# Attention followed by a maxout layer: AV with stationary exponentials, transposes by DMA, six banks for scores, batch 0 in halves

## The chip, the cores and the metric

The kernel runs on one core of one Trainium2 chip. The metric is the time of one execution on the device in microseconds (us). Executions of a kernel are told as the median of the runs. A run more than 1.5% above the fastest of its kernel counts as slow, and comparisons are made between fast runs. Engines: PE is TensorE (matmuls), PEld its weight loads, DVE is VectorE, ACT is ScalarE, POOL is GpSimd, SP is SyncE, which issues DMAs here. "Granted clock" is the share of TensorE's full clock that the throttle let through.

## The reference

```python
# q, k, v: (8, 12, 448, 64) float32
scores = (1 / sqrt(64)) * q @ k^T
m = max(scores);  e = exp(scores - m)
attn = e / (sum(e) + exp(-m) + 1e-9)       # but for the 1e-9: exp(s) / (sum exp(s) + 1)
x = (attn @ v) -> (8*448, 12*64) = (3584, 768)
h = max(x @ w1, x @ w2, x @ w3)            # three 768 x 768 weights
out = h @ w_out                            # (3584, 768) float32
```

## The kernel before

The work is cut into 24 groups of four heads (three groups to a batch). For each group q and k are loaded, transposed on PE, multiplied to scores (keys on partitions, 112 a chunk), and exponentiated on ACT. The exponentials `eT` are the moving operand of AV: four heads sit side by side in 32-column tiles of the PE array. The denominator is a third such product, with ones as weights. Up pieces (a 128x448 tile of `x @ w_i`) and output pieces of the batch before are put between the visits of attention to keep PE busy.

```python
def pair_qk(i):                     # DVE: two heads side by side, for the transposes
    ...
        nc.vector.tensor_copy(out=k16, in_=kf[...]); nc.vector.tensor_copy(out=q16, in_=qf[...])

def transpose_pair(i, pr):          # PE: 8 transposes into a PSUM bank, DVE copies them out
    trT = ps1.tile([128, 2, S], MMDT, tag="bank1", name="trT")
    for n, t16 in enumerate((k16, q16)):
        for c in range(NCH):
            nc.tensor.transpose(out=trT[:, n, ts(c, SC)], in_=t16[:, c, :, :], ...)
    nc.vector.tensor_copy(out=qkT, in_=trT.rearrange("p n s -> p (n s)"))

def av_group(i):
    def col_tiled(weights):         # 16 matmuls, four heads at once in column tiles of 32
        for c in range(NCH):
            for hh in range(GH):
                nc.tensor.matmul(out=bank[32*hh : 32*hh+32, 0:S], lhsT=weights(hh, c),
                                 rhs=eT[:, hh, c, :], start=(c == 0), stop=(c == NCH - 1))
    den = col_tiled(lambda hh, c: ones16[:, :])
    nc.scalar.activation(out=lnd, in_=den[:, 0:S], func=AF.Ln, bias=one_b)
    nc.scalar.activation(out=rb, in_=lnd, func=AF.Exp, bias=ln_lam, scale=-1.0)
    for hf in range(2):
        num = col_tiled(lambda hh, c: v16[:, hh, c, hf::2])
        nc.vector.tensor_tensor(out=xT[b][:, 2*g + hf, :], in0=num[:, 0:S], in1=rb, op=ALU.mult)
...
# PSUM: ps1 = 4 banks (AV, transposes, up, output), ps2 = 2 x 2 banks (scores)
for i in range(NI):                 # 24 groups, four visits each
    ...
    for vi, (pr, cs) in enumerate(visits):
        scores_visit(i, pr, cs)
        # visit 0: up/output pieces, av_group(i - 1), pieces, pair_qk(i + 1)
        # visits 1, 2: pieces, transpose_pair(i + 1, vi - 1), pieces;  visit 3: pieces
```

The softmax here doesn't subtract the row's maximum and nothing guards it: scores larger than these inputs give would overflow.

## Time and profile before

| | before |
|---|---|
| median of the first three runs | 379.88 us |
| PE busy | 358.3 us of a 377.6 us span |
| ACT busy, DVE busy | 194.5 us, 194.7 us |
| time for one group, first AV to first AV, mean of 19 | 14.6 us |

The head of the profile's page of the kernel before: the span, then busy time and share of the span by engine.

```profile
span 377.6 us, 7320 instructions
PE 358.3 (95%) x3120; PEld 172.0 (46%) x3120; DVE 194.7 (52%) x395; ACT 194.5 (52%) x241; POOL 59.4 (16%) x92
```

PE is the bound. The view by windows of the kernel before tells where it is not. The columns are the stretch, then busy time and number of instructions of each engine, the granted clock, the DMA share and GB/s.

```profile
core 0: us, PE busy (x) PEld busy (x) DVE busy (x) ACT busy (x) POOL busy (x), PEclk, DMA share, GB/s
0.00:40.00 40.00, 26.18 (x269) 11.64 (x270) 12.08 (x33) 27.48 (x35) 20.76 (x37) 1.00 1.12 175
...
120.00:160.00 40.00, 40.00 (x364) 18.88 (x360) 22.18 (x46) 22.51 (x29) 6.29 (x9) 1.00 0.49 83
...
350.00:378.00 28.00, 22.91 (x128) 12.18 (x126) 13.16 (x22) 0.00 (x0) 0.00 (x0) 0.98 0.20 57
```

(The DMA share adds up the times of packets and can pass 1.) Outside the first 40 us and the last 28 PE has no idle time to give; only less PE work, or an earlier start, can shorten the kernel. What one group costs on PE is read from the timeline of the kernel before, PE only (start, time until the last of the merged matmuls ends, line, output and inputs, count):

```profile
135.20 1.30 PE L220 MATMUL p_i<-xT,w_124 128*128 128x448 f16 x6
136.34 1.30 PE L220 MATMUL p_i<-xT,w_122 128*128 128x448 f16 x6
137.57 0.55 PE L161 MATMUL stp<-qkT 64*128 64x448 f16 x4
138.05 0.94 PE L190 MATMUL av<-eT,ones_116 112*32 112x448 f16 x16
138.81 1.69 PE L190 MATMUL av<-eT,ld_v 112*32 112x448 f16 x32
140.43 1.31 PE L220 MATMUL p_i<-xT,w_123 128*128 128x448 f16 x6
```

Differences of starts are what counts, as the pipelined ends overlap: six up matmuls take 136.34 - 135.20 = 1.14 us, the AV burst of 48 takes 140.43 - 138.05 = 2.38 us. An up piece that a score visit follows holds PE for 1.23 us (137.57 - 136.34), 0.09 more; there PE changes from the whole array to row tiles.

### The profile page before, as it was taken

The numbers are of one execution on the slowest core, as the hardware profiler recorded it, in microseconds if no ns is written. First come the engines' busy times: TensorE is split into PE (matmuls) and PEld (weight loads), VectorE is DVE, ScalarE is ACT, GpSimd is POOL, SyncE is SP. The second block draws the span as 40 slices with busy tenths as digits, with TensorE's granted clock in tenths as the row PEclk, the third lists the DMA queues.
The fourth block names the chain that finished last, engine by engine and source line by source line (L and its number), as shares of the span: only waits on it lengthen the run. The fifth ranks groups of instructions, "written<-read, shape, count | busy, mean of one in ns | idle before, by whom it ended". The sixth has DMA issues, their size and how long they took to land.

```text
span 377.6 us, 7320 instructions
## 1 busy us (share of the span) xinstructions
PE 358.3 (95%) x3120; PEld 172.0 (46%) x3120; DVE 194.7 (52%) x395; ACT 194.5 (52%) x241; POOL 59.4 (16%) x92
## 2 busy tenths in 40 slices
PE   2777999999999999999999999999999999999995
PEld 1233444544445444454445544454444554445552
DVE  2233545545546546546546555455465465445553
ACT  1879464663655655555555645546555554552000
POOL 8533450220210201202202202202000000000000
PEclk9999999999999999999999999999999999999999
DMA  7999998555508625455236555077010410013005
GB/s 92 185 208 206 204 196 121 73 136 68 73 2 151 111 54 75 60 139 75 32 43 89 126 101 73 6 128 141 2 26 0 128 43 0 2 32 95 2 0 168
DMA packets 40064, 32.71 MB, mean 87 GB/s; under 512 B 2272, under 2 KB 35296, under 8 KB 40032
## 3 DMA queue, kind: packets, MB, share of 16 engines
q0 software_dynamic: 35552, 21.24, 40.8%
q1 hardware_dynamic: 4480, 11.01, 9.8%
q8 instruction: 24, 0.39, 0.5%
q14 instruction: 8, 0.07, 0.0%
HBM read 42.47 MB, written 11.01 MB: 142 GB/s over the span
## 4 chain that ended last, share of the span: by engine, by line
PE 84%; DMA 9%; ACT 2%; POOL 2%; DVE 1%; issue 1%; DVEq 0%; POOLq 0%
PE p_i L220 43%; PE op_ps L241 15%; PE av L190 11%; PE stp L161 10%; PE trT L144 4%; DMA w_123<-in_moe_w_dram 3%; DMA ld_k<-in_k_dram 3%; DMA ld_q<-in_q_dram 2%; DVE xT L206 1%; ACT eT L170 1%; ACT rb L203 1%; ACT lnd L201 1%; POOL ld_q L88 1%; POOL ld_k L88 1%; POOL ld_v L88 0%
## 5 line engine op out<-in xcount | busy, mean ns | idle before, releaser
L170 ACT ACTIVATE eT<-stp 112x896 f16<-112x896 f32 x192 | 164.9, 916 | 145.1 <-PE stp L161 145.1
L230 DVE TENSOR_TENSOR hT<-hT,p_i 128x448 f16<-128x448 f16 x96 | 59.4, 619 | 45.5 <-PE p_i L220 45.1
L206 DVE TENSOR_TENSOR xT<-av,rb 128x448 f16<-128x448 f32 x48 | 27.8, 619 | 70.8 <-ACT rb L203 64.7
L220 PE MATMUL p_i<-xT,w_122 128*128 128x448 f16 x288 | 63.0, 353 | 0.4
L220 PE MATMUL p_i<-xT,w_123 128*128 128x448 f16 x288 | 62.4, 353 | 0.0
L220 PE MATMUL p_i<-xT,w_124 128*128 128x448 f16 x288 | 62.2, 353 | 0.0
L161 PE MATMUL stp<-qkT 64*128 64x448 f16 x384 | 56.3, 364 | 4.9 <-ACT eT L170 4.8
L241 PE MATMUL op_ps<-w_125,hT 128*128 128x384 f16 x336 | 59.5, 326 | 0.0
L88 POOL DMA_DIRECT2D ld_v<-in_v_dram x24 | 16.8, 702 | 192.3 <-PE av L190 126.3
L248 DVE TENSOR_SCALAR o_sb<-op_ps 128x384 f32<-128x384 f32 x56 | 31.2, 557 | 28.5 <-PE op_ps L241 28.4
L241 PEld LDWEIGHTS <-hT 128*128 128x128 f16 x336 | 30.9, 98 | 24.8 <-issue 6.3
L190 PE MATMUL av<-eT,ld_v 112*32 112x448 f16 x768 | 41.8, 361 | 0.0
L228 DVE CAST hT<-p_i 128x448 f16<-128x448 f32 x48 | 29.7, 620 | 19.9 <-PE p_i L220 19.9
L220 PEld LDWEIGHTS <-w_123 128*128 128x128 f16 x288 | 25.9, 98 | 29.6 <-issue 9.2
L220 PEld LDWEIGHTS <-w_124 128*128 128x128 f16 x288 | 26.0, 98 | 28.7 <-issue 7.8
L220 PEld LDWEIGHTS <-w_122 128*128 128x128 f16 x288 | 26.1, 98 | 27.8 <-issue 7.0
L149 DVE COPY qkT<-trT 128x896 f16<-128x896 f16 x48 | 29.5, 615 | 3.1 <-PE trT L144 3.0
L161 PEld LDWEIGHTS <-qkT 64*128 64x128 f16 x384 | 12.0, 94 | 40.9 <-issue 40.3
L190 PEld LDWEIGHTS <-ld_v 112*32 112x32 f16 x768 | 21.0, 99 | 16.8 <-issue 1.7
L190 PE MATMUL av<-eT,ones_116 112*32 112x448 f16 x384 | 23.3, 364 | 0.0
L88 POOL DMA_DIRECT2D ld_q<-in_q_dram x25 | 17.7, 709 | 6.9 <-DMA w_124<-in_moe_w_dram 1.5
L88 POOL DMA_DIRECT2D ld_k<-in_k_dram x25 | 17.6, 703 | 4.4 <-DMA w_123<-in_moe_w_dram 1.1
(305 smaller groups left out, 142.1 us busy)
## 6 DMA issues: line engine op xcount, KB each, us to landing
ld_v<-in_v_dram POOLq DMA_DIRECT2D x24, 224.0 KB, 4.0
ld_q<-in_q_dram POOLq DMA_DIRECT2D x23, 224.0 KB, 4.9
ld_k<-in_k_dram POOLq DMA_DIRECT2D x23, 224.0 KB, 5.9
out_dram<-o_sb SPq DMA_DIRECT2D x8, 336.0 KB, 2.8
out_dram<-o_sb SPq DMA_DIRECT2D x8, 288.0 KB, 2.7
out_dram<-o_sb SPq DMA_DIRECT2D x8, 240.0 KB, 2.8
out_dram<-o_sb SPq DMA_DIRECT2D x8, 192.0 KB, 2.7
w_122<-in_moe_w_dram POOLq DMA_DIRECT2D x3, 384.0 KB, 10.7
```

Source lines behind the costliest of these rows:

```text
L88: nc.gpsimd.dma_start(out=tiles[name][:, h0 : h0 + step].rearrange("p h c d -> p h (c d)"), in_=src[:, h0 : h0 + step],)
L144: nc.tensor.transpose(out=trT[:, n, ts(c, SC)], in_=t16[:, c, :, :], identity=ident16[0:SC, 0:SC],)
L149: nc.vector.tensor_copy(out=qkT, in_=trT.rearrange("p n s -> p (n s)"))
L161: nc.tensor.matmul(out=stp[:, hh, 0:S], lhsT=qkT[hh * D : hh * D + D, c * SC : c * SC + 128], rhs=qkT[hh * D : hh * D + D, S : 2 * S], sta ...
L170: nc.scalar.activation(out=st["eT"][:, 2 * pr : 2 * pr + 2, c, :], in_=stp[0:SC, :, 0:S], func=AF.Exp, scale=scale,)
L190: nc.tensor.matmul(out=bank[32 * hh : 32 * hh + 32, 0:S], lhsT=weights(hh, c), rhs=eT[:, hh, c, :], start=(c == 0), stop=(c == NCH - 1),)
L206: nc.vector.tensor_tensor(out=xT[b][:, 2 * g + hf, :], in0=num[:, 0:S], in1=rb, op=ALU.mult)
L220: nc.tensor.matmul(out=p_i[:, 0:S], lhsT=w_sb[i][:, dc, ts(fc, 128)], rhs=xT[b][:, dc, :], start=(dc == 0), stop=(dc == NDC - 1),)
L228: nc.vector.tensor_copy(out=dst, in_=p_i[:, 0:S])
L230: nc.vector.tensor_tensor(out=dst, in0=dst, in1=p_i[:, 0:S], op=ALU.max)
L241: nc.tensor.matmul(out=op_ps[:, 0:NW], lhsT=hT[bp][:, fc, ts(t, 128)], rhs=wout_sb[:, fc, ts(nh, NW)], start=(fc == 0), stop=(fc == NFC - 1),)
L248: nc.vector.tensor_scalar(out=o_sb[:, ts(nh, NW)], in0=op_ps[:, 0:NW], scalar1=1.0 / LAMBDA, scalar2=None, op0=ALU.mult,)
```

## The change

The intent: take work from PE and shorten the start.

- AV with the exponentials stationary (113 or 112 rows, 128 columns) and v moving, with a 65th value column of constants that gives the denominator, and a 113th row of ones that gives its "+ 1". DVE takes reciprocals and multiplies; ACT loses Ln and Exp.
- AV's result now has queries on partitions, so x must be transposed as well. From group 5 on q and k, and from group 3 on x, are transposed by DMAs issued on SP.
- The pairing copies of q and k go from DVE to POOL, and POOL copies v into the widened buffer.
- PSUM: three score tiles of two banks (AV uses them too), two single banks for all else; three score visits a group for four.
- Batch 0 is done in query halves, so that its up pieces can start earlier.

```diff
-    ps1 = ... bufs=4 ...
-    ps2 = ... bufs=2 ...
+    ps_s = ctx.enter_context(tc.tile_pool(name="ps_s", bufs=3, space=bass.MemoryType.PSUM))
+    ps_b = ctx.enter_context(tc.tile_pool(name="ps_b", bufs=2, space=bass.MemoryType.PSUM))
 ...
+    def transpose_dma(i):
+        for pr in range(GH // 2):
+            t = att_pool.tile([2 * D, 2 * S], MMDT, tag="qkT", name="qkT")
+            for n in range(2):                       # k, then q
+                nc.sync.dma_start_transpose(
+                    out=t[:, n * S : (n + 1) * S].rearrange("p (c r) -> p c r", c=NCH),
+                    in_=paired[i][pr][n].rearrange("p c h d -> p (c h d)"),
+                )
+    def prep_v(i):
+        nc.gpsimd.tensor_copy(out=v_buf[i % NE][0:SC, :, :, 0:D], in_=raw[i].pop("v"))
 ...
+    def av(i, pr, qcs=(0, 1, 2, 3)):
 ...
+                    nc.tensor.matmul(
+                        out=ps[:, hh, j * (D + 1) : (j + 1) * (D + 1)],
+                        lhsT=eF[0:kk, o : o + 128],
+                        rhs=vx[0:kk, h, c, 0 : D + 1],
+                        start=(c == 0), stop=(c == NCH - 1),
+                    )
+        nc.vector.reciprocal(out=rb[:, :, 0:nq], in_=acc[:, :, :, D])
+        nc.vector.tensor_tensor(out=xn[i][...], in0=acc[:, :, :, 0:D], in1=rb[...], op=ALU.mult)
 ...
+    def x_transpose_dma(i):
+        nc.sync.dma_start_transpose(out=xt_tile(b)[...], in_=xn[i].rearrange("p a j h d -> p (a j h d)"))
 ...
+        for vi, units in enumerate(visits):          # three visits, groups 4 to 23
+            scores(i, units)
 ...
+                fill(per / 6)
+                if vi < 2:
+                    av(i - 1, vi)
+                if vi == 1:
+                    x_transpose_dma(i - 1)
+                    if i + 1 < NI and i + 1 >= PE_QK:
+                        transpose_dma(i + 1)
+                fill(per / 6)
```

The last lines: in each group, SP is given the x transpose of the group whose AV has just been issued, and the four transposes that the next group's scores need.

## The prediction

> **What bounds the kernel now.** TensorE. The page gives PE 95% busy of 377.6 us; the window table shows PE busy for all but 0.2 us of each 40 us between 80 and 320 us, at full granted clock. Only the first 40 us are loose (PE 26.2 us busy, ScalarE 27.5, DMA share above 1). The chain of waits is PE for 84%, DMA 9% (its start).
>
> A group of four heads takes 14.6 us (distance of successive AV bursts in the chain). From start-to-start times in the PE timeline: 36 up matmuls at 0.189 us = 6.8; 14 output matmuls at 0.1625 = 2.3; 8 row-tiled score pairs at 0.189 = 1.5; the AV burst 2.4 (48 column-tiled matmuls, four at once); 16 transposes at 0.049 = 0.8; and about 0.1 us each time PE changes between full array and tiles, near 0.8 a group. 24 groups: about 350 us.
>
> **What changes (estimates from those durations).**
> 1. AV: 48 wide matmuls a group become 64 with 128 stationary columns and 65 moving ones. A weight load with a 112-column transpose matmul takes 48.5 ns in the trace, the load hidden, so a pair costs at most that; streaming alone would be some 29 ns. The Trainium skill ("TensorE: Matmul & The Clock Gate", "Back-to-back issue gap") states a floor near 25 ns, but 81 ns for 128-column pairs; this trace contradicts the second. I take 34 ns: 2.2 us a group for 2.3. AV itself hardly pays.
> 2. DMA transposes for groups 5 to 23 remove 19 x 0.8 = 15 us from PE, the critical engine, and two 0.62 us VectorE copies a group.
> 3. Full-array AV and three score visits for four: 9 mode changes become 6: 6 us.
> 4. ScalarE loses Ln and Exp (31 us), VectorE the pair copies (to GpSimd): off the critical path, slack only.
> 5. Batch 0 in halves: up work starts near 22 to 25 us instead of 39. But DMA moved at most about 2 MB per 9.4 us slice, so the second weight lands near 30 us, the third near 35. I expect 6 to 10 us gained; PE dense from about 35 us.
> 6. The ring for up and output pieces falls from four banks to two; a piece takes 1.14 us, its eviction 0.62 plus about 0.3: just enough. I allow 6 us of stalls.
>
> PE work is then about 331 us, plus some 9 us of idle at the start, 5 at the end, 6 of stalls.
>
> **Predicted: 350 us, 8 in 10 between 334 and 369. Faster by over 2%: 0.89; within 2%: 0.07; slower: 0.04.**
>
> **What would show it.** A group period near 13.4 us (13.1 if AV pairs run at 30 ns, 14.3 at 48). AV burst of 64 near 2.2 us. No PE transposes after about 40 us. ScalarE near 166 us, its waits all for PE. First up matmul at 22 to 26 us, its wait ended by a weight DMA.
>
> **What would make it wrong.**
> - AV pairs slower than 45 ns: 15 to 25 us lost.
> - DMA transposes: some 0.69 MB a group in 256-byte rows. At the 261 GB/s of the skill's "DMA: Bandwidth & Descriptors" ("Latency and other measured facts") that is 2.6 us, hidden; no trace shows it yet. Before's packets of about 600 bytes took about 69 ns; if each row cost that, transposes and loads would fill the 16 engines for over a group's period, PE would wait on the transposed q, k or x, and the time would be 370 or more.
> - GpSimd copies late, delaying the transposes.
> - Two banks too few: PE waits for VectorE at every piece.
> - Batch 0 waiting longer for weights.

## The result

| | before | after |
|---|---|---|
| median of 6 runs | 379.76 us | 423.12 us |
| median of the 4 fast runs of after | | 420.90 us |
| span of the profiled run | 377.6 us | 421.8 us |
| PE busy | 358.3 us | 355.0 us |
| PE not busy | 19.3 us | 66.8 us |
| mean granted clock | 0.999 | 0.949 |
| time for one group | 14.6 us | 15.8 us (first scores to first scores, mean of 14) |

The ratio is 1.108 (95% interval 1.102 to 1.114). Ratios here are the mean time of one kernel's fast runs over that of the other's of the same rounds, so not quite the ratio of the medians quoted. Two of the six runs of after counted as slow by their time (424.36 and 427.52 us); the profiled one is fast. Differences to after are taken from 420.90 below; the expectations took 423.

The record of the clock begins at 21.9 us in before and at 24.2 us in after, and the mean counts the time ahead of it as full speed. In after it was not: eight score matmuls of 224 columns take 0.93 us at 20.9 us and 0.56 at 26.1. So clocks are compared from 80 us on.

The page of the kernel after: span and busy times, then its chain of waits by engine.

```profile
span 421.8 us, 8277 instructions
PE 355.0 (84%) x3438; PEld 203.7 (48%) x3438; DVE 181.5 (43%) x343; ACT 165.0 (39%) x193; POOL 133.4 (32%) x200
...
PE 64%; DMA 21%; SPq 7%; DVE 3%; issue 2%; POOL 1%; ACT 1%; ACTq 0%; POOLq 0%
```

PE is busy for almost as long as before, though it was given less work. The windows of the kernel after:

```profile
0.00:40.00 40.00, 21.47 (x265) 12.76 (x266) 14.80 (x37) 13.30 (x15) 26.46 (x43) 0.89 1.15 172
80.00:120.00 40.00, 29.61 (x295) 18.11 (x296) 11.57 (x22) 16.46 (x20) 16.29 (x24) 0.83 0.66 109
120.00:160.00 40.00, 36.90 (x346) 20.18 (x345) 18.29 (x33) 18.81 (x23) 12.76 (x19) 1.00 0.70 114
...
280.00:320.00 40.00, 31.85 (x278) 16.48 (x277) 15.03 (x27) 15.50 (x19) 13.07 (x20) 0.93 0.75 114
```

There is idle time in every stretch, and in some the clock is down. The list of waits of the kernel after (engine and what waited, on what, us in all, times, longest) says for what:

```profile
PE stp L207 <- DMA qkT<-q: 38.8, 19, 5.3
...
PE avp L237 <- POOL vx L194: 11.9, 2, 8.7
```

Score matmuls of all 19 groups that use DMA transposes wait for a transposed q: 38.8 us. The first AV matmuls of batch 0 wait 11.9 us for POOL's copies of v. The timeline of the kernel after over one change of group shows how the first comes about:

```profile
136.42 1.21 PE L237 MATMUL avp<-vx,e 113*128 113x65 f16 x32
...
137.91 0.69 DVE L249 TENSOR_TENSOR xn<-avp,rb 112x512 f16<-112x512 f32 x1
138.63 1.22 SPq L277 DMA_TRANSPOSE xT<-xn  x1
...
139.96 1.20 SPq L186 DMA_TRANSPOSE qkT<-k  x1
141.25 1.21 SPq L186 DMA_TRANSPOSE qkT<-q  x1
142.57 1.20 SPq L186 DMA_TRANSPOSE qkT<-k  x1
143.67 0.74 PE L207 MATMUL stp<-qkT 64*128 64x448 f16 x6 [0.91 <-DMA qkT<-q]
```

The x transpose starts 0.03 us after DVE has made its input. Behind it each issue holds SP for 1.2 us, and the q that the next scores need lands 2.4 us after its issue. From the end of AV's matmuls (136.42 + 1.21) to the scores 6.0 us pass, 0.9 more than the filling work behind AV lasts. The copies of q and k that these transposes read were made a whole group earlier: they wait for their place in the queue, not for data.

### The profile page after: what moved, and what is told of

Same layout as the page of the kernel before. It is cut to its first block, busy times and chain, and to the rows that moved or that the text cites. A ratio compares the mean times of both kernels' runs of the same rounds, so it can differ in the third digit from the quotient of the medians.

```text
span 421.8 us, 8277 instructions
## 1 busy us (share of the span) xinstructions
PE 355.0 (84%) x3438; PEld 203.7 (48%) x3438; DVE 181.5 (43%) x343; ACT 165.0 (39%) x193; POOL 133.4 (32%) x200
## 2 busy tenths in 40 slices
DMA packets 97190, 46.33 MB, mean 110 GB/s; under 512 B 58240, under 2 KB 93568, under 8 KB 97152
## 4 chain that ended last, share of the span: by engine, by line
PE 64%; DMA 21%; SPq 7%; DVE 3%; issue 2%; POOL 1%; ACT 1%; ACTq 0%; POOLq 0%
PE p_i L294 33%; DMA qkT<-q 14%; PE avp L237 12%; PE op_ps L316 9%; PE stp L207 9%; DMA w<-in_moe_w_dram 6%; SPq L186 6%; SPq L277 2%; DMA ld_k<-in_k_dram 1%; DVE hT L305 1%; ACT e L216 1%; DVE xn L249 1%; DVE o_sb L323 1%; POOL ld_k L96 0%; POOL ld_q L96 0%
## 5 line engine op out<-in xcount | busy, mean ns | idle before, releaser
L216 ACT ACTIVATE e<-stp 112x896 f16<-112x896 f32 x192 | 163.7, 916 | 210.4 <-PE stp L207 210.1
L294 PE MATMUL p_i<-xT,w 128*128 128x448 f16 (+1 forms) x972 | 185.0, 341 | 0.6 <-DVE qkT L179 0.3
L294 PEld LDWEIGHTS <-w 128*128 128x128 f16 x972 | 90.6, 100 | 80.4 <-issue 25.5
L207 PE MATMUL stp<-qkT 64*128 64x448 f16 (+1 forms) x432 | 56.4, 360 | 44.4 <-DMA qkT<-q 38.8
L154 POOL COPY k<-ld_k 112x512 f16<-112x512 f16 x42 | 25.9, 618 | 169.1 <-DMA qkT<-k 161.4
L237 PE MATMUL avp<-vx,e 112*128 112x65 f16 (+1 forms) x1536 | 62.1, 198 | 14.2 <-POOL vx L194 11.9
L237 PEld LDWEIGHTS <-e 112*128 112x128 f16 (+1 forms) x1536 | 59.7, 101 | 24.8 <-issue 16.5
L316 PE MATMUL op_ps<-w,hT 128*128 128x384 f16 x336 | 60.0, 330 | 0.0
L249 DVE TENSOR_TENSOR xn<-avp,rb 112x512 f16<-112x512 f32 (+1 forms) x54 | 34.1, 632 | 1.9
L154 POOL COPY q<-ld_q 112x512 f16<-112x512 f16 x42 | 26.0, 618 | 21.3 <-DMA qkT<-q 21.3
```

Of the source, the lines that this page charges most:

```text
L154: nc.gpsimd.tensor_copy(out=t16, in_=f[:, 2 * pr : 2 * pr + 2].rearrange("p h c d -> p c h d"))
L207: nc.tensor.matmul(out=stp[:, hh, j * qn : (j + 1) * qn], lhsT=t[hh * D : hh * D + D, c * SC : c * SC + 128], rhs=t[hh * D : hh * D + D, S ...
L216: nc.scalar.activation(out=eT[0:SC, 2 * pr : 2 * pr + 2, cs[0] : cs[0] + len(cs), q0 : q0 + qn], in_=stp[0:SC, :, 0 : len(cs) * qn].rearra ...
L237: nc.tensor.matmul(out=ps[:, hh, j * (D + 1) : (j + 1) * (D + 1)], lhsT=eF[0:kk, o : o + 128], rhs=vx[0:kk, h, c, 0 : D + 1], start=(c == ...
L249: nc.vector.tensor_tensor(out=xn[i][:, pr, qcs[0] : qcs[0] + nq].rearrange("p j h d -> p h j d"), in0=acc[:, :, :, 0:D], in1=rb[:, :, 0:nq ...
L294: nc.tensor.matmul(out=p_i[:, j * qn : (j + 1) * qn], lhsT=w_sb[i][:, dc, ts(fc, 128)], rhs=xT[b][:, dc, q0 : q0 + qn], start=(dc == 0), s ...
```

## The experiments

All eleven kernels gave correct results. Times are medians; each is compared with the kernel before on the same chip (379.5 to 379.8 us there).

| run | what | us | ratio to before (95%) |
|---|---|---|---|
| (after) | the change | 423.12 (fast: 420.90) | 1.108 (1.102 to 1.114) |
| early | q/k transposes issued after the first scores | 372.19 | 0.981 (0.977 to 0.984) |
| merged | k and q in one DMA | 394.35 | 1.039 (1.036 to 1.043) |
| pe_qk | q/k transposes on PE | 397.45 | 1.046 (1.043 to 1.049) |
| warmgap | idle stretches filled with matmuls | 415.70 | 1.096 (1.090 to 1.102) |
| xlast | x behind q/k, same place | 377.42 | 0.993 (0.990 to 0.997) |
| early_vx | early, v of batch 0 copied on DVE | 358.42 | 0.944 (0.942 to 0.947) |
| early_start | early_vx, buffers cleared later | 363.56 | 0.959 (0.955 to 0.963) |
| early_merged_start | early_start, k and q in one DMA | 365.88 | 0.960 (0.956 to 0.965) |
| xlag | x of the group before last ahead of q/k | 407.14 | 1.072 (1.068 to 1.075) |
| pe_all_vx | every transpose on PE, v on DVE | 396.88 | 1.047 (1.043 to 1.051) |
| xpe | x on PE, q/k by DMA | 388.05 | 1.022 (1.019 to 1.026) |

The theory to start with, A: q and k come late because they are issued late and one after another. Rival B: the DMA engines are too full of 256-byte rows. Rival C: the clock fell for a reason of its own.

### early

```diff
         for vi, units in enumerate(visits):
             scores(i, units)
+            if vi == 0 and i > 3 and i + 1 < NI:
+                transpose_dma(i + 1)
 ...
                     x_transpose_dma(i - 1)
-                    if i + 1 < NI and i + 1 >= PE_QK:
-                        transpose_dma(i + 1)
```

> The four q/k transposes of the next group are issued right after the first scores of the current group, not behind its x transpose; same transposes, same bytes. Theory A (late, serial issue: x, k, q, k, q at 1.2 us each on SyncE, started only after the second AV, then 2.4 us landing): the 38.8 us that score matmuls wait for the transposed q go to under 5 us, the mean granted clock rises from 0.949 to 0.98 or more, and the time falls from 423 to some 375 (365 to 385). Rival B (the DMA engines are too full of 256-byte rows): the landings stay as long, the waits only move, and the time stays above 405. Rival C (the clock throttles for its own reasons): waits gone, but the granted clock stays near 0.95 and the time near 390.

Measured: 372.19 us, 49 less than after. No wait of PE for q or k is left in its list. The windows of early (same columns as before):

```profile
0.00:40.00 40.00, 21.45 (x268) 12.93 (x269) 14.79 (x37) 13.57 (x16) 26.57 (x43) 0.71 1.15 173
80.00:120.00 40.00, 38.70 (x442) 22.76 (x440) 19.51 (x36) 23.83 (x29) 19.14 (x29) 1.00 1.12 146
120.00:160.00 40.00, 39.30 (x399) 21.60 (x396) 19.86 (x37) 20.35 (x24) 13.62 (x21) 1.00 0.98 144
160.00:200.00 40.00, 40.00 (x365) 21.24 (x363) 20.54 (x37) 20.23 (x24) 17.31 (x26) 1.00 0.96 135
```

The same number of DMA packets moved (97,190 in both), at a higher DMA share, and PE waits for no transposed q or k. The landings are long here, a median of 6.0 us for k and 5.5 for q against 2.4 in after, as B foretold, but nobody waits for them: B falls as the cause by itself. The mean clock is 0.966, under the 0.98 expected, but nearly all of the loss lies at the start (0.71 in the first 40 us; after has 0.89 for the same PE work because its record begins later); from 80 us on it is 1.00. C falls too. A group takes 13.38 us (mean of 14), against a predicted 13.4.

### merged

```diff
-            for n in range(2):
-                nc.sync.dma_start_transpose(out=t[:, n*S:(n+1)*S]..., in_=paired[i][pr][n]...)
+            nc.sync.dma_start_transpose(
+                out=t.rearrange("p (c r) -> p c r", c=2 * NCH),
+                in_=paired[i][pr].rearrange("p n c h d -> p (n c h d)"))
```

> k and q of a pair of heads are paired into one tile and transposed by one DMA of twice the size: two issues a group for four, same bytes, same place in the program. In the trace an x transpose of 8 blocks took as long to issue (1.22 us) as a q or k transpose of 4 blocks (1.20 us), so Theory A expects q with the first issue: the wait per group falls by about 1.2 us, 38.8 us to some 16 to 22 us, and the time falls to about 395 (385 to 405). Rival B (bytes or rows bound) expects no change: 415 to 428.

Measured: 394.35 us, as A expected. Twice the bytes in one DMA hold SP for a median of 1.24 us, against 1.21 for one half. The waits of scores for it are 17.8 us. Bytes are the same, so B by itself is against the evidence here as well.

### pe_qk

```diff
-                    if i + 1 < NI and i + 1 >= PE_QK:
-                        transpose_dma(i + 1)
+                if vi > 0 and i + 1 < NI:
+                    transpose_pe(i + 1, vi - 1)
```

> All q/k transposes back on TensorE (x stays on DMA). PE gets 19 groups x 16 transposes x 0.049 = 15 us of work more. Theory A and B both expect the waits for q/k landings gone and the clock back at 0.98 or more: 423 - 39 - about 15 (clock) + 15 = about 384 (374 to 394). If the time stays above 405, the loss is in the AV form, the two PSUM banks or the start, and not in the transposes.

Measured: 397.45 us; the expectation of 384 missed by 13. The waits are gone and the clock is 1.00 from 80 us on, as expected, but transposes on PE cost more than their own time. A group takes 14.73 us, 1.35 more than in early: 0.78 of transposes, and after the second burst of eight in each group PE starts the next piece 0.46 to 0.53 us after the last transpose began, where 0.049 is its normal distance (and what the first burst shows). That is 0.42 to 0.48 us, once a group; the list names DVE's copy out of an earlier piece as the releaser. It is the ring of two banks, in which a short burst leaves no time for DVE's 0.62 us copy. (The expectation of pe_all_vx below spreads the same time over both bursts, as twice 0.24.) So in this kernel, with its ring of two, transposes by DMA that are in time save 25 us and not the 15 predicted.

### warmgap

```diff
         for vi, units in enumerate(visits):
+            if vi == 0 and i >= 5:
+                warm(6)                    # six 512-column matmuls on zeros
             scores(i, units)
```

> Kernel after, with six 512-column matmuls on zeros (about 1.3 us at full clock, result unused) ahead of the first scores of groups 5 to 23, where PE sat waiting. The waits stay, but most of each is filled with work. If the lower granted clock is a cost of its own that follows from the idle stretches, the clock rises to 0.97 or more and the time falls by 4 to 12 us in spite of 25 us of extra PE work; if the clock costs nothing beyond the waits, the time is the same or up to 10 us longer.

Measured: 415.70 us, 5.2 less than the fast runs of after, with 19 x 1.3 = 25 us more of PE work (an estimate from six matmuls at full clock). By time alone that is at the edge of the noise: the intervals of the two ratios just touch (1.090 to 1.102, 1.102 to 1.114). But PE's busy time rose by 13.8 us only (368.8 - 355.0), so all other matmuls together took some 11 us less. The mean clock is 0.957, short of the 0.97 expected, mostly because of the start (0.68); from 120 us on it is 1.00. So the clock is a cost of its own and follows from idle stretches. The kernel after shows it directly, in the timeline behind its longest wait:

```profile
311.69 1.22 SPq L186 DMA_TRANSPOSE qkT<-q  x1
...
318.14 1.30 PE L207 MATMUL stp<-qkT 64*128 64x448 f16 x6 [5.28 <-DMA qkT<-q]
...
319.38 3.29 PE L294 MATMUL p_i<-xT,w 128*128 128x448 f16 x12
```

The six score matmuls last 1.30 us and not the 0.74 seen above, the twelve up matmuls 3.29 us where they otherwise last 2.44. The Trainium skill ("TensorE: Matmul & The Clock Gate", Part 1) puts the clock at half after an idle window of about 3.4 us; this trace agrees on the half and not on the length. Between 80 and 400 us the clock's record in after has eight stretches at half, seven of 3.41 us and one of 6.83, one at the end of each of the eight waits for q of 2.2 us or more (2.20 to 5.28) and none at the eleven of 1.6 us or less; up matmuls that start in them are 0.373 us apart and not 0.189. The record of warmgap has two such stretches in the same time.

The first line also shows a part of rival B. The q issued at 311.69 landed 6.4 us later, not 2.4, so 4.0 us of this wait are a slow landing. Summed over the 19 groups, landings longer than 2.4 us make up 12.4 of the 38.8 us of waits; the rest is the late issue.

### xlast

```diff
-                    x_transpose_dma(i - 1)
                     if i + 1 < NI and i + 1 >= PE_QK:
                         transpose_dma(i + 1)
+                    x_transpose_dma(i - 1)
```

> Kernel after with one order turned: at the same place in the program, the four q/k transposes of the next group are issued first and the x transpose last. Same count, same bytes, same late start. If the waits come from the serial queue ahead of q (Theory A), taking one issue of 1.2 to 1.35 us out of q's way saves about as much a group as merging did, which saved 29 us: about 395 (386 to 403). If the time of landing is the limit and the queue ahead is not, 415 or more.

Measured: 377.42 us, 43 less than after, far more than one issue of 1.2 us a group explains (19 x 1.2 = 23; merged took one away from ahead of q and gained 27). So theory A as stated falls short: neither the place in the program nor the number of issues alone counts. In early and in xlast SP has the same order of transposes (k, q, k, q, x, k, q, ...); only output stores stand differently between. What both changed is that q and k no longer stand behind the x that waits for this group's AV. SP issues in the order of the program; in xlast it issues the first k of group 8 at 101.4 us, 11.2 us ahead of that group's scores, in after at 124.5, 3.7 us ahead. The timelines, xlast and then after:

```profile
101.43 1.39 SPq L186 DMA_TRANSPOSE qkT<-k  x1
...
112.63 0.74 PE L207 MATMUL stp<-qkT 64*128 64x448 f16 x6
```

```profile
124.54 1.20 SPq L186 DMA_TRANSPOSE qkT<-k  x1
...
128.24 0.74 PE L207 MATMUL stp<-qkT 64*128 64x448 f16 x6 [0.89 <-DMA qkT<-q]
```

This gives theory A2: the head of SP's queue waits for a result that PE makes late, and everything behind it waits too. A1 keeps the number of issues as the cause.

### early_vx

```diff
     def prep_v(i):
-        nc.gpsimd.tensor_copy(
+        eng = nc.vector if i < NG else nc.gpsimd
+        eng.tensor_copy(
```

> Version early, with the copies of v for the three groups of batch 0 on VectorE instead of GpSimd, where they stood behind the issues of the weight loads (waits of 3.2 and 8.7 us of the first AV matmuls in the trace of after). Theory of the start (the copies are late because GpSimd issues loads first): both waits go, the first up matmul moves from 41.4 us to 30 to 33 us, and the time falls from 372 to about 364 (358 to 368). Rival (weights land late anyway): the wait moves to a weight DMA and under 3 us are gained.

Measured: 358.42 us, the best of all, 13.8 less than early where 8 were expected. Both waits for v are gone, and the first up matmul starts at 27.98 us instead of 41.20 in early (41.35 in after). The page of early_vx:

```profile
span 356.7 us, 8280 instructions
PE 338.7 (95%) x3438; PEld 195.7 (55%) x3438; DVE 182.8 (51%) x346; ACT 165.0 (46%) x193; POOL 129.5 (36%) x197
```

In after POOL's copy of v for group 2 stood behind issues of k, v and w_out. The timeline of the kernel after:

```profile
28.28 0.70 POOL L96 DMA_DIRECT2D ld_k<-in_k_dram  x1 [1.13 <-DMA w<-in_moe_w_dram]
30.16 0.70 POOL L96 DMA_DIRECT2D ld_v<-in_v_dram  x1 [1.18 <-DMA w<-in_moe_w_dram]
32.04 0.71 POOL L108 DMA_DIRECT2D w<-in_moe_w_out_dram  x1 [1.18 <-DMA w<-in_moe_w_dram]
33.98 0.71 POOL L108 DMA_DIRECT2D w<-in_moe_w_out_dram  x1 [1.22 <-DMA w<-in_moe_w_dram]
35.81 0.71 POOL L108 DMA_DIRECT2D w<-in_moe_w_out_dram  x1 [1.13 <-DMA w<-in_moe_w_dram]
36.52 1.05 POOL L194 COPY vx<-ld_v 112x1024 f16<-112x1024 f16 x1
...
37.62 1.04 PE L237 MATMUL avp<-vx,e 113*128 113x65 f16 x16 [8.73 <-POOL vx L194]
```

Each issue waits about 1.2 us for an earlier weight transfer, so a copy that takes 1.05 us comes some 8 us late. It is the same shape as on SP: an in-order queue whose head waits for something that the work behind it does not need.

### early_start

```diff
-    for j in range(NE):
+    def clear(j):
 ...
+    clear(0)                        # only the first e and v buffers are cleared here
     warm(10)
     transpose_pe(0, 0)
 ...
-            if half == 0 and u == 1:
+            if half == 0 and u == 2:
+                if g < 2:
+                    clear(g + 1)
+            if half == 0 and u == 3:
                 prep_v(g)
```

> As early_vx, and the clearing of the second and third buffers of exponentials moved behind the first transposes on VectorE (in the trace of after the first copy out of PSUM waited until 10.3 us behind the clears, though its transposes were done at 6.5). The first exponential moves from 11.6 us to about 8; up to 3 us more than early_vx, so about 361 (355 to 366).

Measured: 363.56 us, 5 slower than early_vx; the gain I expected is a loss. The first exponential did move, from 11.5 us in early_vx to 6.9. But k and q of group 1 land only at 10.6 and 12.0 us, so PE stopped there (2.0 and 1.0 us), and the clears, now in the middle, held DVE while AV, exponentials and x of batch 0 waited for it (2.2, 2.2 and 2.6 us in its timeline). In early_vx the clears were over by then. The edit also moves the copies of v from the second visit to the fourth; no run separates that from the clears.

### early_merged_start

It is early_start with the edit of merged.

> early_start with k and q of a pair in one transpose DMA. The issues are off the critical path once they are early, so Theory A expects no gain over early_start (within 1%, that is within 3.6 us); if the transposes still limit something, it is faster by more.

Measured: 365.88 us with two of six runs slow; by the fast runs 364.64, 0.3% above early_start, and the ratios' intervals overlap. Once the transposes are in time, the number of issues no longer counts, as expected.

### xlag

```diff
-                    x_transpose_dma(i - 1)
+                    if i - 2 >= 3:
+                        x_transpose_dma(i - 2)
+                    if i >= 7 and i % 3 == 1:
+                        add_batch(i // 3 - 1)      # moved here from the head of the group
+                        per = left() / 2.95
                     if i + 1 < NI and i + 1 >= PE_QK:
                         transpose_dma(i + 1)
```

(The spreading of the pieces over the visits was adapted to the later start of a batch's pieces.)

> Kernel after with the same order of transposes (x first, then k, q, k, q, at the same place), but the x that stands ahead is that of the group before last, which was normalised some 13 us earlier; the up pieces of a batch start half a group later for it. The issue of x (1.2 us) still stands ahead of k and q; only its wait for the fresh AV result is gone. Theory A2 (the in-order SyncE queue is held by the x transpose that waits for this group's AV; xlast and early had both taken that wait out of q's way): the wait of the scores for q is under 8 us in all and the time about 376 (367 to 388). Theory A1 (what counts is the number of issues of 1.2 us ahead of q): the waits stay above 25 us and the time above 405.

Measured: 407.14 us. This fits neither theory whole. The waits of xlag:

```profile
PE p_i L294 <- DMA xT<-xn: 22.6, 6, 7.1
...
PE stp L207 <- DMA qkT<-q: 3.1, 1, 3.1
```

The wait for q fell from 38.8 to 3.1 us with the x issue still ahead of it, which A1 forbids. But up pieces now wait for the late x, and those gaps cost clock again (0.91 in 80 to 120 us). As a test of the time it is confounded; as a test of the wait it speaks for A2.

### pe_all_vx

It is early_vx with the q/k edit of pe_qk, and `x_transpose_pe(i - 1, (0, 1, 2, 3))` in visit 2 for the x transposes.

> early_vx with every transpose, q, k and x, on TensorE and none by DMA: what the transposes by DMA are worth once they are not late. pe_qk lay 25 us above early, 1.33 us a group: 0.78 of transposes and two waits of about 0.24 us for a free bank in the ring of two. Eight x transposes a group add 0.39 + about 0.24 us. Expected 358 + 25 + 21 x 0.63 = about 396 (388 to 404). If it is under 380, the transposes by DMA are worth less than thought.

Measured: 396.88 us, as expected. Without DMA transposes the change loses to the kernel before even with its start mended: the new AV brings a transpose of x, and with two banks PE waits at the short bursts. In this form transposes by DMA carry the change, 38 us of it (396.88 - 358.42), these waits included; PE transposes with a ring of four banks were not run.

### xpe

```diff
-                    x_transpose_dma(i - 1)
                     if i + 1 < NI and i + 1 >= PE_QK:
                         transpose_dma(i + 1)
+                if vi == 2:
+                    x_transpose_pe(i - 1, (0, 1, 2, 3))
```

> Kernel after with the x transposes of groups 3 to 23 on TensorE and the q/k transposes by DMA at their place of after. No x transpose stands in the SyncE queue, so nothing in it waits for the AV of this group; output stores remain. xlag had exchanged the wait for q for one for x, so this asks the same without x in the queue. PE work grows by 21 x 0.63 = 13 us. Theory A2 (the queue is held by the x that waits for its AV): waits for q under 5 us, 372 + 13 = about 385 (376 to 394). Theory A1 (issues ahead of q only): one issue of 1.3 us a group less, so some 394 + 13 = 407 (400 to 416).

Measured: 388.05 us, in A2's range and far below A1's. PE and PEld wait for no transposed q or k at all, where after had 38.8 us of such waits. The four q/k issues are where they were in the program; only the x that waited in front of them is gone. A2 stands.

Moving x to another queue, so that it could wait without holding anyone, was not tried. The Trainium skill ("Advanced Engine Details and Errata", "X-Bar Transpose (TRN2)") warns that transposes from two queues in flight together silently corrupt each other; no run here shows it.

## Why the prediction was wrong

Predicted were 350 us (334 to 369) and a gain; measured 423.12 and a loss. The direction was wrong because of SP's queue, and POOL's cost another 13.8 us; the sum of PE work was near (about 331 us predicted, 338.7 busy in early_vx, where both queues are mended).

- **AV pairs at 34 ns: right.** Start to start the AV matmuls take 32.7 ns in early, 2.1 us a group.
- **Group period of 13.4 us: right where nothing waits.** early shows 13.38, after 15.8.
- **Mode changes: right.** A score visit starts 0.285 us after an up matmul, and an up matmul 0.282 us after a score visit, where 0.189 is normal; there are three visits a group.
- **The DMA transposes "remove 19 x 0.8 = 15 us from PE" and themselves take "2.6 us, hidden": hidden is the step that failed.** They do remove that PE work, and with the bank waits 25 us (pe_qk against early). But I costed only the removed work, and took the new operation as overlapped. In after it was not: PE waited 38.8 us for a transposed q, and the granted clock fell in the gaps. The size of the two together is what early gives back: 51.8 us between the profiled runs (421.8 - 370.0), of which PE's idle time accounts for 38.0 (66.8 - 28.8) and slower matmuls for 13.8 (355.0 - 341.2).
- **The risk was named, but mainly for the wrong reason.** I feared that 256-byte rows would fill the DMA engines. They take a median of 18 ns each in after and in early_vx, against the 69 ns that I feared. Slow landings made up 12.4 us of the waits of after; yet in early_vx the median landing takes 5.6 us instead of 2.4, with more traffic around it, and nobody waits, as the transposes are early. What turned landings into waits was the order of SP's queue: an x transpose that waits for this group's AV, ahead of the q and k that the next scores need. The order of the issues, which was at hand in the program before the run, has x first, and x is written by DVE after AV; I did not ask what stood behind that wait.

The DMA list of early_vx, with the median time from issue to landing, shows the landings:

```profile
qkT<-k SPq DMA_TRANSPOSE x38, 5.6
qkT<-q SPq DMA_TRANSPOSE x38, 5.5
```

and of after:

```profile
qkT<-k SPq DMA_TRANSPOSE x38, 2.4
qkT<-q SPq DMA_TRANSPOSE x38, 2.4
```

- **Batch 0 "6 to 10 us gained; PE dense from about 35 us": wrong in after.** The first up matmul started at 41.35 us, not at 22 to 26, and the wait before it was for POOL's copy of v and not for a weight. With the copy on DVE it started at 27.98 and 13.8 us were gained.
- **Two banks with "6 us of stalls": too careful here.** In after and early PE does not wait for DVE between up pieces (in early_vx an up matmul starts 0.190 us after the one before, as in before). The ring costs only where short transposes pass through it.
- **ScalarE 165.0 us: right, and off the path**, as said.

With both queues mended the kernel takes 358.42 us, within the predicted range, 8 above the middle. PE's busy time is 338.7 us for 331 and its idle time 18.0 for 20, so both terms of the sum hold, to 8 us and to 2. How much of the loss in after belongs to the clock alone is not separated by a run. The slower matmuls say 13.8 us, and the eight stretches at half clock (30.7 us, so at most 15.4 lost) fit that; warmgap regained 5 us net of the work that it added.

## What to carry to other kernels

An operation moved from a busy engine to a DMA is free only if its result is in time, so write down for each in-order queue what stands ahead of it and what that head waits for. A transfer whose input is old should be issued ahead of one whose input is the newest result of the bound engine; here exchanging two calls was worth 43 us. The same holds for a compute engine that also issues loads: a short copy behind throttled issues comes as late as they do.

## What the Trainium skill lacked or had wrong

- "TensorE: Matmul & The Clock Gate", "Back-to-back issue gap": it gives about 81 ns for pairs of weight load and matmul of 128 columns. The nearest shape here, transposes of 112 columns, runs at 49 ns a pair; pairs with a 65-column matmul, about half as wide, run at 32.7 ns. No pair of exactly 128 columns was run.
- The same page's Part 1 ties the half clock to an idle window of about 3.4 us; here waits of 2.20, 2.20, 2.60 and 3.04 us brought it too.
- "TensorEngine Tiling (Array Packing)" says that a change of tiling mode drains TensorE, without a price: 0.093 us a change here (0.282 against 0.189 us).
- "DMA: Bandwidth & Descriptors" gives a rate for DMA transposes ("Latency and other measured facts", 261 GB/s), but no time for their issue that is measured on trn2: each held SP for a median of 1.21 us, and 1.24 us for twice the bytes. The rate itself agrees: in the busiest microsecond of the trace of after, 1,007 rows of 256 bytes were started, 258 KB, so some 258 GB/s.
- The rules of "DMA: Bandwidth & Descriptors" ("Rules for kernel authors") advise issuing a DMA early and waiting late. They do not say that a DMA early in the program is still late if one ahead of it on the same issuing engine waits: here that was worth 43 us (xlast).
